# Issuing the next head pair's q and k transposes one group per block, in blocks 0, 1 and 2

## The chip, the cores and the metric

The kernel runs on one core of one Trainium2 chip. The metric is the device time of one execution in microseconds (us), as a median over runs. The engines are TensorE (PE), VectorE (DVE), ScalarE (ACT), GpSimd (POOL) and SyncE (SP, which here only issues DMAs).

## The reference

Rotary attention, whose result is flattened into tokens for a gated feed-forward layer (all in fp32):

```python
q_rot, k_rot = (rotate(q), rotate(k))              # q, k, v: (B 4, H 8, S 576, D 64)
scores = np.matmul(q_rot, k_rot.transpose(0, 1, 3, 2)) / np.sqrt(D)
scores = scores - np.max(scores, axis=-1, keepdims=True)
attn = np.exp(scores)
attn = attn / (np.sum(attn, axis=-1, keepdims=True) + 1e-09)
o = np.matmul(attn, v)
x = np.ascontiguousarray(o.transpose(0, 2, 1, 3)).reshape(B * S, H * D)   # (2304, 512)
g = x @ w_gate                                     # w_gate, w_val: (512, 1536)
out = (g * (1.0 / (1.0 + np.exp(-g))) * (x @ w_val)) @ w_out              # w_out: (1536, 512)
```

## The kernel before

The 32 heads are treated as 16 head pairs, p = 0 to 15. A pair has nine blocks, b = 0 to 8, so attention is 144 blocks, n = 9p + b. Blocks 0 to 7 are one 128-row tile of queries of one head of the pair (heads alternate); block 8 holds the 64 remaining rows of both heads. The feed-forward layer starts behind attention, and takes the last 60% of the span.

A number is kept as the sum of two halves, hi and lo, so that TensorE's fast pass keeps precision; every product is made of several passes over such halves.

A block goes through these steps. `scores` (L349): four matmuls into a PSUM tile `sc`, of which there are two buffers. DVE takes the row maximum from it (L364, `nmt`), ACT the exponential (L382, `E`, or `Et` for block 8, and behind it a short read of the accumulated sum). This exponential is the last reader of the `sc` buffer. PE transposes E (L425; the tails of 64 columns at L435 and L437) into a PSUM tile `tr`, of which there are three buffers; ACT casts that to the hi half (L426, `ET1h` or `ET2h`; L440 `TK1h`, `TK2h`), and DVE subtracts it to make the lo half (L427 and L441, `ET2l`, ...), which is the last reader of the `tr` buffer. Then PE multiplies by V (L465, `pv`), one half of a pair's query tiles at a time, and ACT copies the output out (L470, `Y`).

The next head pair is prepared beside that. SP loads q and k of a head pair into `X` (L175, `load_qk`; two buffers, so the load of pair p+2's `X` waits until POOL has read that of pair p). POOL rotates it (`rope`, L206 to L208) into `rot`; the last instruction of a head pair that reads `X` is its second big L207. In pair p, `qk_T` is called three times for pair p+1: once each for the 512 columns of q, the 512 of k, and the tails of both. A call is four transposes of PE (L289; two at L293 for the tails) into a `tr` buffer, a cast of ACT (L308, `N`), and a subtraction of DVE (L312). The last call also calls `qk_stack`, which issues eight DMAs on SP that copy `N` into the stacked tiles that the scores of pair p+1 read: `QK` (L319 and L320 for the first head, L322 and L323 for the second), `QZ` (L321, L324) and `BD` (L325, L326). Block 0 of pair p+1 needs the first head's part, block 1 the second's.

In which block of a pair the three calls are made is a row of the plan, `PLAN["qk"]`: one row for pair 0, one for pair 1 and one for pairs 2 and later. `PLAN["qkw"]` says what each call treats: for pairs from 1 on, the tails, then q, then k. The step that reads them:

```python
    def qk(n, p, b):
        w, bs = P["qkw"][min(p, 2)], P["qk"][min(p, 2)]
        if p + 1 < NP:
            for i in range(3):
                if bs[i] == b:
                    at.qk_T(p + 1, w[i], i == 2)
```

`load_qk(p + 3)` is called in block 2 of pairs 2 to 5 and in block 0 of pair 1 and of pairs 6 to 12 (L1065), ahead of the block's steps. The instructions of PE, ACT and DVE are ordered by a list scheduler with a model of their times; those of POOL stand as written all through attention, those of SP as written up to block 47 and by the scheduler from then on (pair 5 begins with block 45).

Of the kernel before, what the change touches and what calls it, by code (L numbers as in the profile page):

```python
# [28 lines left out]
    trb=3,  # L29
    warm=[9, 0, 1, 2, 0, 1],  # L30
    order=["qk", "scores", "trans", "pv", "exp", "evac", "rstore", "rope", "tails", "conv", "x", "conv1", "vsplit"],
    qk=[[3, 4, 6], [1, 2, 3], [0, 0, 1]],
    qkw=[[0, 2, 1], [2, 0, 1], [2, 0, 1]],
    tails=[4, 0],
    pv=[1, 6, 5, 3, 7, 8, 2, 7, 3],
# [1471 lines left out]
```

## Time and profile before

| | |
|---|---|
| time, median of 3 runs | 690.47 us (690.37 to 690.92) |
| time of the profiled execution | 690.11 us |
| its span in the trace | 688.3 us, so 1.8 us lie outside the span |
| busy share of the span | PE 98%, DVE 85%, POOL 68%, ACT 62% |
| attention's scores run from, to | 19.2 us, 272.2 us |

PE's share counts a matmul as busy until its modelled end, so a short wait of PE can lie hidden in it; waits are better read from the distance between the starts of its instructions than from idle time. Times in the rows are microseconds from the start of the span.

### The profile page before, as it was taken

To read this page: it belongs to the slowest core of one execution; us is meant where nothing else is said; L and a number is where in the kernel's file an instruction comes from. 1 tells how busy PE (TensorE), PEld (TensorE's weight loads), DVE (VectorE), ACT (ScalarE), POOL (GpSimd) and SP (SyncE) were. 2 spreads that over 40 slices of the span, in tenths; PEclk is the share of its full clock that TensorE was granted. 3 is DMA by queue.
4 is the path that set the end of the run, shared out by engine and by line. 5 is a ranking of instruction groups with operands and counts; after the bars stand their busy time and mean duration, and the time that the engine had idled before them with its cause. 6 is when DMAs were issued, how large, how long until landed. Compare 5 with 4: busy or idle time off the path is not lost. (4 is left out here: it accounts for less than half of the span.)

```text
span 688.3 us, 12675 instructions
## 1 busy us (share of the span) xinstructions
PE 677.4 (98%) x4414; PEld 664.3 (97%) x4414; DVE 582.4 (85%) x883; ACT 424.2 (62%) x873; POOL 470.1 (68%) x475
## 2 busy tenths in 40 slices
PE   7999999999999999999999999999999999999998
PEld 6899999999999999999999999999999999999997
DVE  5888898888888888979988898988999599877683
ACT  5899988888888888555543434424435375344341
POOL 8899799999999985998889588677784720000000
PEclk9999999999999999999999999999999999999999
DMA  6897999889988879791214345354464797627101
GB/s 195 185 248 205 218 225 243 208 206 243 246 206 208 220 189 285 187 235 70 90 58 164 122 141 204 130 187 150 161 212 163 264 317 252 207 74 247 47 24 69
DMA packets 78784, 125.76 MB, mean 183 GB/s; under 512 B 16880, under 2 KB 55680, under 8 KB 78720
## 3 DMA queue, kind: packets, MB, share of 16 engines
q1 hardware_dynamic: 75248, 118.77, 60.6%
q10 hardware_dynamic: 3472, 6.18, 2.4%
q8 instruction: 35, 0.57, 0.4%
q14 instruction: 29, 0.24, 0.1%
HBM read 66.91 MB, written 33.10 MB: 145 GB/s over the span
## 5 line engine op out<-in xcount | busy, mean ns | idle before, releaser
L364 DVE TENSOR_REDUCE nmt<-sc 128x1 f32<-128x576 f32 x144 | 108.2, 751 | 20.3 <-PE sc L349 18.9
L382 ACT ACTIVATE E<-sc,nmt 128x576 f32<-128x576 f32 x128 | 97.5, 761 | 1.7 <-DVE nmt L364 1.6
L425 PE MATMUL tr<-ident,E 128*128 128x128 f32 x512 | 77.1, 274 | 0.4 <-DVE ET1l L427 0.2
L425 PEld LDWEIGHTS tr<-ident,E 128*128 128x128 f32 x512 | 61.2, 141 | 3.4 <-PE tr L289 1.3
L1472 PE MATMUL ch<-dW,dO 128*128 128x384 f32 x216 | 63.8, 337 | 0.2 <-DVE dW L1420 0.2
L206 POOL TENSOR_TENSOR t<-X,tab 128x256 f32<-128x256 f32 (+2 forms) x94 | 54.4, 600 | 9.4 <-DMA X<-in_qk_dram 5.8
L349 PE MATMUL sc<-QK 128*128 128x288 f32 x240 | 58.7, 325 | 1.4 <-ACT E L382 0.6
L426 ACT CAST ET2h<-tr 128x512 fp32r<-128x512 f32 x80 | 47.2, 590 | 14.0 <-PE tr L425 13.7
L427 DVE TENSOR_TENSOR ET2l<-tr,ET2h 128x512 fp32r<-128x512 f32 x80 | 53.1, 682 | 2.1 <-ACT ET2h L426 2.0
L349 PE MATMUL sc<-N,QZ 128*128 128x288 f32 x240 | 51.3, 296 | 0.0
L695 POOL TENSOR_TENSOR W<-WF,W 128x1024 fp32r<-128x1024 f32 x20 | 48.1, 2409 | 3.8 <-ACT W L695 3.7
L208 POOL TENSOR_TENSOR rot<-rot,t 128x512 f32<-128x512 f32 (+2 forms) x47 | 47.0, 999 | 3.7
L427 DVE TENSOR_TENSOR ET1l<-tr,ET1h 128x512 fp32r<-128x512 f32 x64 | 43.0, 685 | 7.0 <-ACT ET1h L426 6.7
L207 POOL TENSOR_TENSOR rot<-X,tab 128x512 f32<-128x512 f32 (+2 forms) x47 | 47.0, 1001 | 0.0
L1472 PE MATMUL ch<-dH,dO 128*128 128x384 f32 x156 | 45.5, 337 | 0.0
L426 ACT CAST ET1h<-tr 128x512 fp32r<-128x512 f32 x64 | 36.9, 597 | 13.1 <-PE tr L425 13.1
L842 PE MATMUL ch<-T2h,W 128*128 128x384 f32 x160 | 44.2, 337 | 0.0
L842 PE MATMUL ch<-T0h,W 128*128 128x384 f32 x160 | 44.2, 337 | 0.0
L842 PE MATMUL ch<-T1h,W 128*128 128x384 f32 x160 | 44.1, 336 | 0.0
L465 PE MATMUL pv<-ET2h,VS 128*128 128x320 f32 x128 | 40.8, 329 | 1.1 <-ACT ET2h L426 0.9
L349 PEld LDWEIGHTS sc<-QK 128*128 128x128 f32 x240 | 36.9, 190 | 4.3 <-ACT E L382 4.1
L1472 PEld LDWEIGHTS ch<-dW,dO 128*128 128x128 f32 x216 | 39.8, 188 | 0.5 <-DVE dW L1420 0.5
(349 smaller groups left out, 2300.7 us busy)
## 6 DMA issues: line engine op xcount, KB each, us to landing
QK<-N SPq DMA_DIRECT2D x64, 288.0 KB, 4.3
hd<-sg SPq DMA_DIRECT2D x14, 768.0 KB, 3.3
dB<-hd SPq DMA_DIRECT2D x8, 1152.0 KB, 7.3
X<-in_qk_dram SPq DMA_DIRECT2D x15, 576.0 KB, 5.6
yd<-Y SPq DMA_DIRECT2D x31, 256.0 KB, 5.7
raw<-in_moe_w_gate_dram SPq DMA_DIRECT2D x12, 512.0 KB, 3.7
raw<-in_moe_w_val_dram SPq DMA_DIRECT2D x12, 512.0 KB, 4.0
Xab<-yd SPq DMA_DIRECT2D x32, 192.0 KB, 4.9
```

Of the source, the lines that this page charges most:

```text
L206: e.tensor_tensor(out=sel(t2, u), in0=sel(x, w), in1=tb(Sn, u), op=ALU.mult)
L207: e.tensor_tensor(out=o, in0=x, in1=tb(C, slice(0, D)), op=ALU.mult)
L208: e.tensor_tensor(out=o, in0=o, in1=t2, op=ALU.add)
L349: nc.tensor.matmul(ps[:, g, 0:288], l, rr[:, o + g * 288:o + (g + 1) * 288], start=(x == 0), stop=(x == len(terms) - 1))
L364: nc.vector.tensor_reduce(out=nmcol, in_=ps[:, :, 0:288], axis=AX.XY, op=ALU.max, negate=True)
L382: nc.scalar.activation(out=E.rearrange("p (a b) -> p a b", a=2), in_=ps[:, :, 0:288], func=ACTF.Exp, bias=nmcol, scale=1.0, accum_out=self ...
L425: nc.tensor.transpose(ps[:, c], E[:, o + c * 128:o + (c + 1) * 128], self.ident)
L426: nc.scalar.copy(dst[0], src)
L427: nc.vector.tensor_tensor(out=dst[1], in0=src, in1=r32(dst[0]), op=ALU.subtract)
L695: return [lambda: self.nc.scalar.copy(h, f), lambda: le.tensor_tensor(out=l, in0=f, in1=r32(h), op=ALU.subtract)]
L842: nc.tensor.matmul(acc, l[:, w, c * 128:(c + 1) * 128], r, start=(n == 0 and k not in ONTO), stop=(n == 5), skip_group_check=True)
L1472: nc.tensor.matmul(ps, l, r[:, f], start=(new and f == 0 and x == 0), stop=(f == NFP - 1 and x == 2), skip_group_check=True)
```

## The change

The three calls of `qk_T` go to blocks 0, 1 and 2, one each, in every pair from 1 on. In pair 1 each stands one block earlier than before; in pairs 2 and later the tails stay in block 0, q goes from block 0 to block 1, and k, with the eight DMAs of `qk_stack`, from block 1 to block 2.

```diff
-    qk=[[3, 4, 6], [1, 2, 3], [0, 0, 1]],
+    qk=[[3, 4, 6], [0, 1, 2], [0, 1, 2]],
```

The number of instructions is the same on each engine; what differs is their order within attention. The steps of a block work ahead: in block n the scores and the exponential are those of block n+1. Order of PE in block 0 and 1 of a pair, before (the first row is the last product by V that belongs to the block ahead; `sc<-QK` with `sc<-N,QZ` are one block's scores, here of blocks 1, 2 and 3; `Et` is block 8 of the pair ahead):

```order
L465 MATMUL pv<-TK1l,VS_115 128x256
L349 MATMUL sc<-QK_112 128x288 x2
L349 MATMUL sc<-N_111,QZ_114 128x288 x2
L289 MATMUL tr<-ident,rot 128x128 x4
L425 MATMUL tr<-ident,Et 128x128 x4
L349 MATMUL sc<-QK_112 128x288 x2
L349 MATMUL sc<-N_111,QZ_114 128x288 x2
L435 MATMUL tr<-ident,E 128x128 x2
L437 MATMUL tr<-ident,Et 128x2x64
L349 MATMUL sc<-QK_112 128x288 x2
L349 MATMUL sc<-N_111,QZ_114 128x288 x2
L289 MATMUL tr<-ident,rot 128x128 x4
```

and PE of the change at the same place:

```order
L465 MATMUL pv<-TK1l,VS_115 128x256
L293 MATMUL tr<-ident,rot 128x128 x2
L349 MATMUL sc<-QK_112 128x288 x2
L349 MATMUL sc<-N_111,QZ_114 128x288 x2
L425 MATMUL tr<-ident,Et 128x128 x4
L349 MATMUL sc<-QK_112 128x288 x2
L349 MATMUL sc<-N_111,QZ_114 128x288 x2
L435 MATMUL tr<-ident,E 128x128 x2
L437 MATMUL tr<-ident,Et 128x2x64
L465 MATMUL pv<-ET2h,VS_115 128x320
L289 MATMUL tr<-ident,rot 128x128 x4
L349 MATMUL sc<-QK_112 128x288 x2
```

The q transposes went from behind the scores of block 1 to just ahead of those of block 3, and one product by `ET2h` now stands ahead of them; the k transposes, in the last row of before, follow later, behind the scores of block 4.

Order of ACT there, before (from the copy of the block-8 tails to the second `ET1h`):

```order
L385 COPY Et<-Et 128x64
L382 ACTIVATE E,sumt<-sc,nmt 128x576
L470 COPY Y_2460<-pv 128x256
L308 CAST N_91<-tr 128x512
L382 ACTIVATE E,sumt<-sc,nmt 128x576
L426 CAST ET2h<-tr 128x4x2x64
L440 CAST TK2h<-tr 128x384
L382 ACTIVATE E,sumt<-sc,nmt 128x576
L308 CAST N_91<-tr 128x512
L426 CAST ET1h<-tr 128x4x128
```

and ACT of the change:

```order
L385 COPY Et<-Et 128x64
L382 ACTIVATE E,sumt<-sc,nmt 128x576
L470 COPY Y_2460<-pv 128x256
L308 CAST N_91<-tr 128x3x64
L426 CAST ET2h<-tr 128x4x2x64
L382 ACTIVATE E,sumt<-sc,nmt 128x576
L440 CAST TK2h<-tr 128x384
L382 ACTIVATE E,sumt<-sc,nmt 128x576
L308 CAST N_91<-tr 128x512
L426 CAST ET1h<-tr 128x4x128
```

The cast of q (128x512) no longer stands ahead of the exponential of block 1 (the second `L382` row); the casts of the tails (128x3x64) and of `Et` do.

Order of SP, the piece of the difference in pair 5, where the stack of pair 6 is issued:

```order
-L319 DMA QK_92<-N_91 64x2x576
-L320 DMA QK_92<-N_91 64x2x576
-L321 DMA QZ_94<-N_91 64x512
-L322 DMA QK_92<-N_91 64x2x576
-L323 DMA QK_92<-N_91 64x1152
-L324 DMA QZ_94<-N_91 64x512
-L325 DMA BD_93<-N_91 64x2x64
-L326 DMA BD_93<-N_91 64x2x64
-L175 DMA X<-in_qk_dram 128x1152
-L489 DMA yd_57<-Y_1561 128x2x256
-L490 DMA yd_57<-Y_1561 128x2x64
-L175 DMA X<-in_qk_dram 128x1152
```

```order
+L175 DMA X<-in_qk_dram 128x1152 x2
+L319 DMA QK_92<-N_91 64x2x576
+L320 DMA QK_92<-N_91 64x2x576
+L321 DMA QZ_94<-N_91 64x512
+L322 DMA QK_92<-N_91 64x2x576
+L323 DMA QK_92<-N_91 64x1152
```

The two loads of `X` went from behind the stack to ahead of it. In pairs 2 to 4 one load of `X` does the same. In pair 6 the load of head pair 10's `X` goes from behind the four `QK` DMAs to ahead of them; from pair 7 on it stands behind them in both.

## Rows read from the trace of the kernel before

**Rows 1.** Windows, a steady stretch: busy us by engine, granted clock, DMA share, GB/s.

```profile
150.00:200.00 50.00, 49.68 (x394) 48.45 (x393) 43.73 (x71) 44.39 (x114) 47.82 (x57) 1.00 0.92 236
```

**Rows 2.** Timeline of PE, start of pair 11: start, duration, engine, line, tiles, count.

```profile
195.50 0.43 PE L349 MATMUL sc<-QK 128*128 128x288 f32 x2
...
197.68 0.27 PE L437 MATMUL tr<-ident,Et 128*128 128x128 f32 x1
198.05 0.52 PE L349 MATMUL sc<-QK 128*128 128x288 f32 x2
...
198.68 0.60 PE L289 MATMUL tr<-ident,rot 128*128 128x128 f32 x4
199.03 0.39 PE L465 MATMUL pv<-ET2h,VS 128*128 128x320 f32 x1
199.40 0.63 PE L425 MATMUL tr<-ident,E 128*128 128x128 f32 x4
...
201.04 0.42 PE L349 MATMUL sc<-QK 128*128 128x288 f32 x2
```

**Rows 3.** Timeline of PE in pair 0, the same sequences without a wait.

```profile
29.12 0.27 PE L437 MATMUL tr<-ident,Et 128*128 128x128 f32 x1
29.15 0.50 PE L349 MATMUL sc<-QK 128*128 128x288 f32 x2
...
33.03 0.39 PE L465 MATMUL pv<-TK2l,VS 128*128 128x320 f32 x1
33.27 0.49 PE L425 MATMUL tr<-ident,E 128*128 128x128 f32 x3
```

**Rows 4.** Timeline of ACT, start of pair 11; brackets show idle time and releaser.

```profile
196.68 0.59 ACT L308 CAST N<-tr 128x512 fp32r<-128x512 f32 x1 [0.19 <-PE tr L289]
197.16 0.75 ACT L382 ACTIVATE E<-sc,nmt 128x576 f32<-128x576 f32 x1
197.80 0.20 ACT L382 ACTIVATION_READ_ACCUMULATOR E<-sc,nmt 128x1 f32 x1
```

**Rows 5.** Timeline of DVE, start of pair 11.

```profile
196.24 0.76 DVE L364 TENSOR_REDUCE nmt<-sc 128x1 f32<-128x576 f32 x1
...
198.57 0.68 DVE L427 TENSOR_TENSOR ET2l<-tr,ET2h 128x512 fp32r<-128x512 f32 x1
```

**Rows 6.** Timeline of PE: a stall in pair 4, scores of pairs 6 and 7.

```profile
81.58 0.41 PE L465 MATMUL pv<-ET2h,VS 128*128 128x320 f32 x1 [0.88 <-ACT ET2h L426]
...
113.02 0.43 PE L349 MATMUL sc<-QK 128*128 128x288 f32 x2
...
127.03 0.51 PE L349 MATMUL sc<-QK 128*128 128x288 f32 x2
...
129.48 0.42 PE L349 MATMUL sc<-QK 128*128 128x288 f32 x2
```

**Rows 7.** Timeline of SP, DMA issues of pairs 3 and 6.

```profile
74.46 0.59 SPq L175 DMA_DIRECT2D X<-in_qk_dram  x1
...
118.81 0.61 SPq L319 DMA_DIRECT2D QK<-N  x1
...
121.10 1.27 SPq L323 DMA_DIRECT2D QK<-N  x1
123.66 0.33 SPq L175 DMA_DIRECT2D X<-in_qk_dram  x1
```

**Rows 8.** Timeline of POOL: the rope of head pairs 6, 7 and 8.

```profile
80.12 0.60 POOL L206 TENSOR_TENSOR t<-X,tab 128x64 f32<-128x64 f32 x2 [3.76 <-DMA X<-in_qk_dram]
...
103.95 1.29 POOL L207 TENSOR_TENSOR rot<-X,tab 128x512 f32<-128x512 f32 x1
...
122.33 1.30 POOL L207 TENSOR_TENSOR rot<-X,tab 128x512 f32<-128x512 f32 x1
```

**Rows 9.** DMA issues in 109 to 110: count, KB each, us to landing.

```profile
X<-in_qk_dram SPq DMA_DIRECT2D x1, 576.0 KB, 4.4
```

**Rows 10.** All DMAs that write tile QK.

```profile
DMA to landing us min/median/max: 3.2/4.3/7.1
```

## The prediction

> **What bounds the kernel now.** I read the page first, for the shares of the engines, and then the windows of a steady stretch of attention: in 50 us PE is busy 49.68 at a granted clock of 1.00, POOL 47.82, and the DMA engines carry 236 GB/s at a share of 0.92 [rows 1]. So PE sets the pace at its full clock, POOL and the DMAs follow closely, and DVE and ACT have some room. A change that adds and removes no instruction can only win back PE's waits. These lie hidden in its busy time, so the timeline is to be read by the distance between starts. From the scores of block 1 in pair 7 (129.48) to those in pair 11 (195.50) there are four pairs in 66.02 us, 16.5 each [rows 2, 6].
>
> In each such pair there are two waits at its start. **The first:** the lone transposes of L437 start at 197.68 and the scores behind them at 198.05, 0.37 later; without a wait the same two rows stand 0.03 apart [rows 2, 3]. That is 0.34. The scores waited for their `sc` buffer, which the exponential of block 1 frees. On ACT that exponential starts at 197.16, directly behind the cast of q (196.68), which itself had to wait 0.19 for its transposes; its maximum on DVE was done at 196.24 + 0.76 = 197.00 [rows 4, 5]. So the q cast, not the maximum, is what came last. **The second:** `pv` starts at 199.03, the transposes behind it at 199.40, 0.37 against 0.24 without a wait [rows 2, 3]. That is 0.13. They waited for a `tr` buffer, which the subtraction of `ET2l` frees at 198.57 + 0.68 = 199.25 [rows 5]; the q group took one of the three buffers, and the block-8 group stood behind it. Together 0.47 us a pair, which is all that this change can give in a steady pair.
>
> **The change, part by part.** No instruction is added or removed on any engine, so the feed-forward part costs the same and shifts with attention's end. Four things move.
>
> *The q group, in pairs from 2 on, to behind the scores of block 2.* Ahead of the third scores (of block 3) PE now has the same work as before and one product more. Before, they were ready 0.34 ahead of 198.05, that is 2.21 after the scores of block 1 at 195.50; with the 0.24 of that product [rows 3] it is 2.45. When is the buffer free? On ACT the cast of block 8 takes the place of the q cast, behind transposes that stand in the same place, so I let the exponential start as before, 197.16 - 195.50 = 1.66 after those scores; it released the third scores 198.05 - 197.16 = 0.89 later [rows 2, 4]. So the buffer is free at 2.55, and the wait is 0.10 where it was 0.34: 0.24 saved. The second wait goes, because the block-8 group now comes first and its buffer is free long before: 0.13 saved. The sum is 0.37 a pair. The bounds are 0 (the exponential comes 0.24 later, behind the tail cast that now also stands ahead of it) and 0.47 (the exponential follows its maximum at once).
>
> *Which pairs keep it.* Pairs 8 and 12 have the extra transposes and copies of the row sums in the same place, with a wait of their own; I count nothing for them. Pairs 15 and 0 prepare nothing or are unchanged. Pairs 7, 9, 10, 11, 13 and 14 remain, six: 6 x 0.37 = 2.2, bounds 0 and 6 x 0.47 = 2.8.
>
> *The k group and the stack, one block later.* k's transposes stood at 198.68 and now follow the scores of block 4, at 201.04 with some 0.5 for those [rows 2]; less the 0.35 of their own length and the 0.37 saved, that is about 201.04 + 0.5 - 0.35 - 0.37 - 198.68 = 2.1 us later. The second head's last `QK` DMA is issued at 121.10 in pair 6 and needed at 129.48 [rows 6, 7]: 8.38 ahead, less 2.1 is 6.3. Such a DMA lands after 4.3 in the median and 7.1 at most [rows 10]. So 2.0 of cover are left in the median case, and the worst costs 0.8 in one pair. I take nothing, since the six pairs' slack repeats and the median fits; without that cover each pair would lose what it lacks.
>
> *The loads of X, ahead of the stack, up to pair 6.* This is the part with a sign that must be weighed. First what it gives: head pair 6's X was issued at 74.46, behind a stack, and POOL stood 3.76 for it at 80.12 [rows 7, 8]. Issued ahead, this wait goes; since POOL is busy 47.82 in 50, all that follows on POOL comes about 3.76 earlier. Then what it costs: a load of X can wait for POOL to have read the buffer's old contents, and on SP all that is queued behind it waits too. For head pair 10's load that read ends at 122.33 + 1.30 = 123.63, and the load went at 123.66 [rows 7, 8]. With POOL's gain it goes at 119.9. It lands 4.4 later [rows 9], at 124.3. The four `QK` DMAs of pair 7 now stand behind it. At 236 GB/s [rows 1] each of 288 KB takes 294,912 B / 236 GB/s = 1.25 (an estimate): the second is there at 126.8, the fourth at 129.3. The scores that read them start at 127.03 and 129.48 [rows 6]. So if these transfers queue behind X, only 0.2 us of what PE may have gained in pairs 1 to 6 survives pair 7. If they go beside X, the last is issued 2.29 + 0.6 (the distance from 118.81 to 121.10, and X's own issue) after 119.9 and lands 4.3 later, at 127.1: then 2.4 survive. For pair 6 the load of head pair 9 waits for 103.95 + 1.29 = 105.24, less 3.76 is 101.5; with 4.4 and four times 1.25 the last lands at 110.9, against 113.02 [rows 6, 8], so there 2.1 could survive. Since the DMA engines are at 0.92, I take the first case, 0.2, and round it to nothing.
>
> The Trainium skill, "DMA: Bandwidth & Descriptors", section "Anatomy of one DMA", gives for a transfer issued by GpSimd 2.0 us plus the bytes at 436 GB/s, which for X's 589,824 bytes is 3.35 us (an estimate); the row above has 4.4 on SP's queue. By that figure X lands 1.05 earlier and about 1.2 us of the gain of pairs 1 to 6 would survive, for 687.1 us; the measured row decides here.
>
> **The sum.** The profiled execution took 690.11, the median is 690.47; a saving does not depend on which, and the profiled one would come to 690.11 - 2.2 = 687.9. From the median: 690.47 - 2.2 = 688.3 us.
>
> **The rivals.** *Full gain.* The transfers of pair 7 go beside X and the early pairs' waits are won too, such as the 0.88 of PE at 81.58 [rows 6]. For it: POOL's 3.76 goes for certain if X is early. Against it: the DMA share of 0.92. It gives 2.2 + 2.4 = 4.6, so 685.9 us.
>
> *The wait only moves.* The q cast leaves the exponential of block 1, but it and the k cast now stand ahead of later exponentials, and each is 0.59 long on ACT [rows 4]. If one of these exponentials then frees its `sc` buffer 0.37 too late, the pair gains nothing; the tail cast ahead of block 1's exponential works the same way. For it: two `sc` buffers leave every score behind the exponential two blocks ahead. Against it: later in the pair products by V stand between two scores, 1.6 us from 199.40 to 201.04 [rows 2], so that an exponential has more time there than at the start. It gives 690.5 us.
>
> *Slower: pair 7 waits behind X.* If POOL does not come 3.76 earlier, because it meets another wait on the way to the rope of head pair 8, the load goes at 123.66 as before, X lands at 128.1 and the fourth `QK` at 133.1, 3.6 after 129.48 [rows 6, 7, 9]. With the steady saving that is 690.47 + 3.6 - 2.2 = 691.9 us. It decides the sign from the point where the load goes later than about 119.9 + 0.2 + 2.2 = 122.3. For it: the load has to wait on SP. Against it: POOL's work itself does not change. The same page of the Trainium skill, in the same section, says that a DMA engine does not wait on semaphores and the sequencer that issues does. The trace agrees: the load's issue stands 0.03 behind POOL's last read [rows 7, 8], and all that is behind it on SP stands too.
>
> **How the numbers follow.** The forecast has a chance of 0.36, the full gain 0.15, the moved wait 0.29, the wait behind X 0.20. The time is that of the first, 688.3. About 0.2% (1.4 us) is what a measurement of this kernel can tell from no change: faster is below 689.1, slower above 691.85. The forecast's own range, with its bounds of 0 to 0.47 a pair, is 687.7 to 690.5, and a part of it, with most of the moved wait, falls in "same"; full gain and nearly all the rest of the forecast make faster 0.50, same 0.31, slower 0.19. The range of 8 in 10 runs from the full gain to the slower rival, 685.6 to 691.9, and leaves out half of the latter and little at the lower end.
>
> **What would show it.** Right: in pairs 9 to 14 the third scores stand about 0.13 behind the transposes ahead of them, the period falls from 16.5 to 16.1, POOL's rope of head pair 6 starts without a wait, and PE waits a little for `QK` DMAs in pair 7, where the trace's gain is back at nothing. Wrong: scores that wait for an exponential elsewhere in the pair, waits of PE for a DMA in pairs 3 to 6 or in the steady ones, or a load of X later than 122.3.

## The result and the profile after

The changed kernel takes 696.68 us (median of 6 runs, 695.2 to 699.35), where the kernel before takes 690.66 in the same comparison (6 runs, 689.76 to 691.17). The ratio is 1.0093 [1.0073, 1.0113]: slower by 0.9%, some 6.0 us, where 688.3 was forecast and 691.9 was the upper end. The profiled execution took 697.94 us, 7.8 more than the profiled one of before.

From the page: the span, the shares of the engines, and the group of the scores that read `QK`, with the idle time ahead of it.

```profile
span 696.2 us, 12731 instructions
...
PE 677.3 (97%) x4414; PEld 665.4 (96%) x4414; DVE 585.9 (84%) x883; ACT 426.7 (61%) x873; POOL 470.8 (68%) x475
...
L349 PE MATMUL sc<-QK 128*128 128x288 f32 x240 | 58.9, 326 | 6.3 <-DMA QK<-N 5.6
```

PE stood 5.6 us for `QK` DMAs. The prediction had wanted to see at most a small wait of this kind, in pair 7. The steady stretch answers to [rows 1]:

```profile
150.00:200.00 50.00, 49.13 (x393) 48.24 (x392) 44.35 (x73) 44.81 (x114) 47.28 (x57) 1.00 0.87 225
```

The clock is the same, and PE carries as much work (393 matmuls in 50 us, before 394); so the steady stretch is not where the time went. The timeline of PE shows where:

```profile
94.09 0.40 PE L349 MATMUL sc<-N,BD 128*128 128x288 f32 x1 [1.18 <-ACT E L382]
...
100.63 0.44 PE L435 MATMUL tr<-ident,E 128*128 128x128 f32 x2 [0.85 <-DVE ET2l L427]
...
131.60 0.50 PE L349 MATMUL sc<-QK 128*128 128x288 f32 x2 [1.34 <-DMA QK<-N]
...
152.33 0.27 PE L400 MATMUL tr<-ident,rt 128*36 128x128 f32 x1 [0.41 <-DVE rt L393]
...
153.20 0.41 PE L435 MATMUL tr<-ident,E 128*128 128x128 f32 x2 [0.45 <-DVE N L312]
...
183.63 0.38 PE L349 MATMUL sc<-QK 128*128 128x288 f32 x1
...
199.85 0.50 PE L349 MATMUL sc<-QK 128*128 128x288 f32 x2
...
201.73 0.41 PE L465 MATMUL pv<-ET2h,VS 128*128 128x320 f32 x1
201.98 0.60 PE L289 MATMUL tr<-ident,rot 128*128 128x128 f32 x4
202.46 0.53 PE L349 MATMUL sc<-QK 128*128 128x288 f32 x2
...
266.97 0.50 PE L349 MATMUL sc<-QK 128*128 128x288 f32 x2 [3.49 <-DMA QK<-N]
```

Setting the same scores of the two traces side by side gives how much later each stands (differences of the unrounded times):

| scores | before | the change | later by |
|---|---|---|---|
| block 8 of pair 0 | 23.34 | 24.20 | 0.86 |
| block 1 of pair 4 | 78.46 | 79.12 | 0.66 |
| block 2 of pair 5 | 97.48 | 100.94 | 3.45 |
| block 1 of pair 7 | 129.48 | 133.98 | 4.50 |
| block 1 of pair 14 | 245.08 | 249.40 | 4.33 |
| block 0 of pair 15 | 259.08 | 266.97 | 7.9 |

The first 0.86 is not the change's: at that point both kernels have run the same instructions, and over all the traces below this start lies between 0.24 earlier and 0.86 later than before. Behind it there are three places of loss. The end of pair 4 and the start of pair 5 cost 2.8, of which the first two waits above are 2.0. The start of pair 7 costs about 1.4. The start of pair 15 costs 3.6, nearly all of it the last wait. In between, seven pairs win only 0.17 net, and the feed-forward part adds nothing in this trace. The profiled execution is 1.3 slower than the median, so not all of these are there each time; the section on five traces of one order, below, shows which are.

The DMA issues of SP, first the last `QK` DMA and the first L772 of the kernel before, then the change at pair 7 and at the last stack:

```profile
252.63 1.34 SPq L323 DMA_DIRECT2D QK<-N  x1
...
260.90 0.57 SPq L772 DMA_DIRECT2D raw<-in_moe_w_gate_dram  x1
```

```profile
122.46 0.35 SPq L175 DMA_DIRECT2D X<-in_qk_dram  x1
122.91 0.62 SPq L319 DMA_DIRECT2D QK<-N  x1
...
255.47 0.35 SPq L772 DMA_DIRECT2D raw<-in_moe_w_gate_dram  x1
255.88 1.61 SPq L772 DMA_DIRECT2D raw<-in_moe_w_val_dram  x1
257.58 0.62 SPq L319 DMA_DIRECT2D QK<-N  x1
258.29 0.62 SPq L320 DMA_DIRECT2D QK<-N  x1
...
261.75 1.06 SPq L630 DMA_DIRECT2D R<-rd  x1
```

L772 (`rawload`) loads a 512 KB piece of the feed-forward weights. Before, the last `QK` DMAs went at 250.32 to 252.63 and the first L772 at 260.90, behind them and behind `R<-rd`, the row sums' reciprocals (L630). Now two of these loads stand ahead of the `QK` DMAs. The DMAs issued from 257.5 to 261, with KB each and the median us to landing:

```profile
QK<-N SPq DMA_DIRECT2D x4, 288.0 KB, 8.7
```

Before, the same four landed after 5.6 (here and below, the median of those of the four whose landing the trace has: two before, four in the change). The scores of pair 15 could have started at 266.97 - 3.49 = 263.48. The second `QK` DMA of its first head was issued at 258.29 and landed 8.5 later, at 266.8; the scores started at 266.97.

For the end of pair 4, DVE before, then DVE (with the subtraction of k's lo half in pair 14 as the last row), POOL and ACT of the change:

```profile
88.99 1.20 DVE L754 TENSOR_SCALAR raw<-raw 128x512 uint32<-128x512 uint32 x1
90.11 0.74 DVE L364 TENSOR_REDUCE nmt<-sc 128x1 f32<-128x576 f32 x1
```

```profile
90.67 1.78 DVE L754 TENSOR_SCALAR raw<-raw 128x512 uint32<-128x512 uint32 x1
92.37 1.41 DVE L364 TENSOR_REDUCE nmt<-sc 128x1 f32<-128x576 f32 x2
...
256.10 0.69 DVE L312 TENSOR_TENSOR N<-tr,N 128x512 fp32r<-128x512 f32 x1 [0.30 <-ACT N L308]
```

```profile
90.59 1.58 POOL L279 TENSOR_TENSOR VS<-VR,VS 128x640 fp32r<-128x640 f32 x1
```

```profile
93.21 0.74 ACT L382 ACTIVATE E<-sc,nmt 128x576 f32<-128x576 f32 x1 [0.62 <-DVE nmt L364]
```

A step of the weight conversion (L754, 1.78 us) stands ahead of two maxima; the exponential waits for its maximum, and PE's scores of block 8 wait for the exponential. Before, that step (88.99, 1.20 us) was followed by one maximum alone, and PE did not wait. The length of the step is POOL's doing. Alone it takes 0.41. Here it starts 0.08 behind the start of POOL's L279, which ends at 90.59 + 1.58 = 92.17, and it ends 0.28 after that, at 92.45. In the 16 traces this step stands 52 times in and just behind attention; 32 times it took over 0.44, and each time it ended 0.28 after the end of the POOL instruction that ran when it started.

POOL, the start and the end of ropes, and a wait between two of them, answers to [rows 8]:

```profile
76.59 0.60 POOL L206 TENSOR_TENSOR t<-X,tab 128x64 f32<-128x64 f32 x2
...
101.21 1.28 POOL L207 TENSOR_TENSOR rot<-X,tab 128x512 f32<-128x512 f32 x1
...
109.16 0.73 POOL L278 TENSOR_SCALAR VS<-VR 128x640 fp32r<-128x640 f32 x1 [1.55 <-PE pv L465]
...
121.15 1.29 POOL L207 TENSOR_TENSOR rot<-X,tab 128x512 f32<-128x512 f32 x1
```

POOL's wait of 3.76 for the `X` of head pair 6 is gone. The last read of head pair 7's `X` comes 2.7 us earlier, that of head pair 8's only 1.2 (123.63 before, now 122.44), where 3.76 was forecast: POOL now waits twice for PE's products, 0.81 at 89.78 and 1.55 at 109.16.

### The profile page after: what moved, and what is told of

Same layout as the page of the kernel before. It is cut to its first block, busy times and chain, and to the rows that moved or that the text cites. A ratio compares the mean times of both kernels' runs of the same rounds, so it can differ in the third digit from the quotient of the medians.

```text
span 696.2 us, 12731 instructions
## 1 busy us (share of the span) xinstructions
PE 677.3 (97%) x4414; PEld 665.4 (96%) x4414; DVE 585.9 (84%) x883; ACT 426.7 (61%) x873; POOL 470.8 (68%) x475
## 4 chain that ended last, share of the span: by engine, by line
PE 78%; DVE 8%; DMA 7%; POOL 3%; issue 2%; ACT 2%; SPq 0%; ACTq 0%; DVEq 0%; POOLq 0%
PE ch L842 28%; PE ch L1472 14%; PE pv L465 10%; PE sc L349 9%; PE ch L794 7%; PE tr L425 6%; DMA QK<-N 3%; PE tr L289 2%; DMA yd<-Y 2%; DVE dB L1410 1%; DVE nmt L364 1%; DMA dO<-od 1%; ACT E L382 1%; PE tr L435 1%; DVE dO L1391 1%
## 5 line engine op out<-in xcount | busy, mean ns | idle before, releaser
L364 DVE TENSOR_REDUCE nmt<-sc 128x1 f32<-128x576 f32 x144 | 108.0, 751 | 27.8 <-PE sc L349 26.9
L382 ACT ACTIVATE E<-sc,nmt 128x576 f32<-128x576 f32 x128 | 97.1, 759 | 7.9 <-DVE nmt L364 7.9
L427 DVE TENSOR_TENSOR ET2l<-tr,ET2h 128x512 fp32r<-128x512 f32 x80 | 53.7, 680 | 2.2 <-ACT ET2h L426 1.8
L207 POOL TENSOR_TENSOR rot<-X,tab 128x512 f32<-128x512 f32 (+2 forms) x47 | 47.0, 999 | 0.0
L427 DVE TENSOR_TENSOR ET1l<-tr,ET1h 128x512 fp32r<-128x512 f32 x64 | 42.8, 684 | 4.1 <-ACT ET1h L426 3.8
```

The source lines that it names most:

```text
L364: nc.vector.tensor_reduce(out=nmcol, in_=ps[:, :, 0:288], axis=AX.XY, op=ALU.max, negate=True)
L382: nc.scalar.activation(out=E.rearrange("p (a b) -> p a b", a=2), in_=ps[:, :, 0:288], func=ACTF.Exp, bias=nmcol, scale=1.0, accum_out=self ...
L427: nc.vector.tensor_tensor(out=dst[1], in0=src, in1=r32(dst[0]), op=ALU.subtract)
```

## The experiments

**Theory:** the loss has two main causes. The scheduler puts weight loads ahead of the last stack, supposedly since SP is idle there while it waits for k, which comes one block later; and the end of pair 4 has a DVE step in a worse place. **Rivals:** k one block later is enough by itself to make the `QK` DMAs late; or the loss lies at the end in `R<-rd`, which feeds POOL; or the early loss comes from `X`.

All kernels have the old row in the plan, so pair 0 and the pairs not named are as before; one line of the step `qk` gives the named pairs the new row:

```diff
-        w, bs = P["qkw"][min(p, 2)], P["qk"][min(p, 2)]
+        w, bs = P["qkw"][min(p, 2)], [0, 1, 2] if p in PAIRS else P["qk"][min(p, 2)]
```

Below only `PAIRS` or, where pair 14 gets a row of its own, the expression is shown.

### The last stack: pair 14 alone

**Pair 14 as before, all else changed.**

```diff
+ p in (1, 2, 3, 4, 5, 6, 7, 8, 9, 10, 11, 12, 13)
```

> The changed kernel, but pair 14 (which prepares pair 15) keeps its old row: k and the stack in block 1, so that SP issues the four QK copies ahead of the two weight loads (L772). Theory W (the two weight loads ahead of the QK copies cost the 3.49 us wait at 266.97): the wait goes, 696.7 - 3.5 = 693.2 us. Rival K (the stack issued one block later is enough to be late): also 693.2, since both are undone. Rival A (PE is late at pair 15 for what piled up before, and would wait for something else): 696.7.

It took 698.21, ratio 1.0112 [1.0096, 1.0128]. The wait of pair 15 is gone, yet nothing is won. The scheduler has now put both L772 and the first two loads of L780, more weights, between the stack and `R<-rd`, which goes at 263.37, and POOL waits for it:

```profile
274.40 1.02 POOL L645 TENSOR_TENSOR Xab<-Xab,R 128x384 f32<-128x384 f32 x1 [6.04 <-DMA R<-rd]
```

The loss comes back in the feed-forward part, which needs what POOL makes here. An old row in pair 14 does not bring the old order of SP back.

**Pair 14 with k in block 2, tails and q in block 1.** No weight load stands ahead of the stack here.

```diff
+ [0, 1, 2] if 0 < p < 14 else [1, 1, 2] if p == 14 else P["qk"][0]
```

> The changed kernel with the row 1, 1, 2 in pair 14: k and the stack still in block 2, as changed, but the order that comes of it has no weight load ahead of the QK copies. W: the wait goes nearly whole, 693.2 us, within 0.5. K: the wait of some 3.5 us stays, 696.7.

It took 697.08, ratio 1.0094 [1.008, 1.0109]. By its time alone this speaks for the rival, k's delay. By its trace it does not: the `QK` DMAs land after 5.3 in the median and no scores of pair 15 wait for them. So k in block 2 is not enough for that wait. The time goes elsewhere: POOL waits 7.24 for `Xab<-yd`, DVE 1.90 for POOL ahead of a maximum (273.56), and the scores at 276.43 wait 1.69 for the exponential behind it.

**Pair 14 with tails and q in block 0, k in block 2.** One weight load stands ahead of the stack.

```diff
+ [0, 1, 2] if 0 < p < 14 else [0, 0, 2] if p == 14 else P["qk"][0]
```

> The changed kernel with the row 0, 0, 2 in pair 14: k and the stack in block 2, with one weight load (512 KB) ahead of the QK copies in place of two. W: the wait falls by what one load takes, 524,288 B at 236 GB/s = 2.2 us, to about 1.3: 694.5 us. K: 696.7.

It took 693.9, ratio 1.0048 [1.0036, 1.006]. PE in pair 15:

```profile
262.34 0.50 PE L349 MATMUL sc<-QK 128*128 128x288 f32 x2 [0.92 <-DMA QK<-N]
...
264.98 0.50 PE L349 MATMUL sc<-QK 128*128 128x288 f32 x2 [0.26 <-DMA QK<-N]
```

**Only pair 14 changed.** Two weight loads stand ahead of the stack.

```diff
+ p in (14,)
```

> The kernel before, with the changed row in pair 14 alone: two weight loads ahead of the QK copies, all else as before. W and K: 690.5 + 3.5 - 0.3 = 693.7 us, and one wait of PE for QK at the start of pair 15. A: 690.2, the saving of one pair.

It took 693.02, ratio 1.003 [1.002, 1.004], so this pair alone costs 2.1 us. PE in pair 15 waits 1.22 + 0.92 = 2.14:

```profile
262.85 0.50 PE L349 MATMUL sc<-QK 128*128 128x288 f32 x2 [1.22 <-DMA QK<-N]
...
264.98 0.50 PE L349 MATMUL sc<-QK 128*128 128x288 f32 x2 [0.92 <-DMA QK<-N]
```

**Pair 14 with q and k both in block 1.** `QK` and `R<-rd` both go ahead of all weight loads.

```diff
+ [0, 1, 2] if 0 < p < 14 else [0, 1, 1] if p == 14 else P["qk"][0]
```

> The changed kernel with the row 0, 1, 1 in pair 14: the order that comes of it on SP has the QK copies and both R<-rd loads ahead of all four weight loads, as the kernel before has it. Theory S (the loss at the end of attention is the order of SP's transfers: weights ahead of QK, or weights ahead of R): neither wait, 696.7 - 3.5 = 693.2 us. Rival: any kernel with the row in pair 13 loses some 6 us at the end of attention whatever SP's order is, 696 to 698, as in the two runs with k back in block 1 or with 1, 1, 2.

It took 693.28, ratio 1.005 [1.003, 1.007]: about 3 us of the 6 are back (1.0093 - 1.005 = 0.43%), as expected. SP, the last `QK` DMA, the first `R<-rd` and the first weight load, and behind it the four `QK` DMAs with their median time to landing:

```profile
256.10 1.38 SPq L323 DMA_DIRECT2D QK<-N  x1
...
260.58 0.62 SPq L630 DMA_DIRECT2D R<-rd  x1
...
265.15 0.55 SPq L772 DMA_DIRECT2D raw<-in_moe_w_gate_dram  x1
```

```profile
QK<-N SPq DMA_DIRECT2D x4, 288.0 KB, 5.7
```

Together (cover is the time from the issue of the first `QK` DMA to where the first scores of pair 15 were otherwise ready, that is their start less their wait):

| kernel | weight loads ahead | landing, median | cover | PE's waits |
|---|---|---|---|---|
| the change | 2 | 8.7 | 5.9 | 3.49 |
| only pair 14 | 2 | 9.4 | 8.65 | 1.22, 0.92 |
| 0, 0, 2 | 1 | 8.2 | 7.85 | 0.92, 0.26 |
| 0, 1, 1 | 0 | 5.7 | 8.1 | none |
| 1, 1, 2 | 0 | 5.3 | 7.0 | none |
| pairs 4 and 5 as before (0, 1, 2 in pair 14) | 0 | 4.2 | 7.1 | none |

In the 13 traces without loads ahead (before and twelve experiments, some of them below) these DMAs land after 4.2 to 7.2 in the median, with loads ahead after 8.2 to 9.4. That, and not k's block, makes the wait: in 1, 1, 2 and in the last run of all, with pairs 4 and 5 as before, k stands in block 2 too, and PE does not wait. The cover, which is not the same in the three kernels with loads ahead although k stands in block 2 in all of them, sets how much of the landing shows. In the change itself k's lo half was done at 256.10 + 0.69 = 256.79 and SP was busy with the second load until 255.88 + 1.61 = 257.49, so 0.8 of the cover went there too.

**Five traces of one order.** The change and the four kernels above that keep its rows up to pair 13 (pair 14 as before; 1, 1, 2; 0, 0, 2; 0, 1, 1) have the same instructions in the same order on every engine up to the scores of block 0 of pair 14. So up to there their traces are five executions of one program, and show what belongs to the order and what to the execution. The loss from block 1 of pair 4 to block 2 of pair 5 is 2.75 to 2.80 in all five. Pairs 7, 10 and 11 win 0.22 to 0.30 each in all five. The wait of pair 7 is in the change's trace alone: in the other four `X` stands ahead of the stack as well, but the first `QK` DMA lands after 5.5 to 5.9 (7.4 in the change), and PE does not wait. Pair 8 loses 0.61 in the change and wins 0.16 or 0.17 in the other four; pair 12 loses 0.38 to 0.61 in four and wins 0.17 in one. And PE waits 0.61 to 1.33 for `QK` at the start of pair 2 in four of the five.

**Only pair 13 changed.**

```diff
+ p in (13,)
```

> The kernel before with the changed row in pair 13 alone. On SP the only part of note that follows is that the two loads R<-rd of pair 15 go from ahead of the four weight loads (L772 twice, L780 twice) to behind them. Theory R (as in the run with pair 14 as before, POOL waits for R and the feed-forward part starts late): 690.7 - 0.3 + 5 to 6 = 695.5 to 696.5 us, with a wait of POOL for R of 5 to 6 us near 272. Rival: that loss belonged to pair 14's row alone, and this gives 690.4.

It took 697.73, ratio 1.0096 [1.0081, 1.011]: one steady pair, which should have won 0.37, costs 6.8 us. Attention ends 0.26 earlier than before; all is lost behind it. SP, and POOL:

```profile
256.83 0.54 SPq L772 DMA_DIRECT2D raw<-in_moe_w_gate_dram  x1
...
258.97 1.67 SPq L780 DMA_DIRECT2D raw<-in_moe_w_gate_dram  x2
261.63 1.26 SPq L630 DMA_DIRECT2D R<-rd  x2
```

```profile
272.66 1.02 POOL L645 TENSOR_TENSOR Xab<-Xab,R 128x384 f32<-128x384 f32 x1 [6.01 <-DMA R<-rd]
```

Before, `R<-rd` went at 257.04, ahead of all of these. From 300 to 350 us PE is now busy 46.62 of 50, before 50.00. So the feed-forward start hangs on the same order of SP, by a second thread.

### The steady pairs

**Pairs 7, 9, 10 and 11.**

```diff
+ p in (7, 9, 10, 11)
```

> The kernel before with the changed row in pairs 7, 9, 10 and 11 alone; SP's order around the end of attention is that of before. The prediction's step for a steady pair (0.37 us saved) gives 690.7 - 1.5 = 689.2 us; what the traces of the changed kernels show for these pairs (about 0.25 a pair) gives 689.7; a rival by which the k stack one block later makes QK late in a steady pair gives a loss, above 690.7.

It took 691.85, ratio 1.0011 [1.0003, 1.002]: no gain. Pairs 7 and 9, each behind an unchanged pair, win 0.43 and 0.44; pairs 10 and 11 win 0.02 each. Pairs 8 and 12, unchanged behind changed ones, give back 0.47 and 1.06; the longest wait of PE there stands at 213.38:

```profile
213.38 0.44 PE L425 MATMUL tr<-ident,Et 128*128 128x128 f32 x2 [0.81 <-DVE ET2l L427]
```

So this kernel does not isolate the steady saving: it has borders that the change has not. No run shows that saving by its time; it is read from the traces of the kernels with all these pairs changed.

**Pairs 8 and 12**, with the row sums:

```diff
+ p in (8, 12)
```

> The kernel before with the changed row in pairs 8 and 12 alone, those with the row sums. Prediction: nothing, 690.7. By the changed kernel's trace each loses 0.5 to 0.6 (PE waits for the reciprocal and for the tails' subtraction): 691.8. By two of the other traces a pair of this kind gains 0.17: 690.4.

690.53, ratio 0.9997 [0.9985, 1.0009]: nothing, as the prediction had it.

**Pairs 2, 3, 8 and 12.**

```diff
+ p in (2, 3, 8, 12)
```

> The kernel before with the changed row in pairs 2, 3, 8 and 12, the ones in which the traces of the changed kernels show no loss; SP's order around the end of attention is that of before. By those traces 0.4 us for pairs 2 and 3 together and 0.2 each for 8 and 12: 690.9 - 0.8 = 690.1 us. Rival (each place where the two rows meet costs some 0.5, as in the run of four steady pairs): 691.9.

691.35, ratio 1.0013 [1.0003, 1.0023]: no gain here either.

### The early pairs

**Pairs 1 to 5.**

```diff
+ p in (1, 2, 3, 4, 5)
```

> The kernel before with the changed row in pairs 1 to 5 alone (the X loads go ahead of the stack there, and the weight conversion of DVE meets other neighbours in pairs 4 and 5). Theory E (the order of DVE and ACT in pairs 4 and 5 loses what the traces of the changed kernels show, some 2.4 us by the start of pair 6): 693.1 us, with PE waiting for the exponential at the end of pair 4 and for ET2l at the start of pair 5, and no wait for QK. Theory of the prediction (a gain that pair 7 takes back): 690.7. A rival by which the X loads make QK late: waits of PE for QK in pairs 2 to 6.

693.45, ratio 1.0049 [1.0032, 1.0066]: the size that was expected. The two waits at the end of pair 4 are there with the lengths that they have in the change, 1.18 at 95.60 and 0.85 at 102.14. The profiled execution, at 695.3 slower than the median, also has two waits for `QK` in pair 2, of 1.29 and 1.08.

**Pair 1.**

```diff
+ p in (1,)
```

> The kernel before with the changed row in pair 1 alone, where it issues the stack of pair 2 one block earlier. Rival of theory E (the QK copies issued earlier meet the loads of X and V and land later): a wait of PE for QK of 0.8 to 2.4 us at the start of pair 2, 691.5 to 693. Theory E: 690.9 or a little less.

690.91, ratio 1.0008 [1.0, 1.0017]: the wait for pair 2's `QK` is not due to pair 1's row alone.

**Pairs 4 and 5.**

```diff
+ p in (4, 5)
```

> The kernel before with the changed row in pairs 4 and 5 alone. Theory E (all of the early loss lies where DVE converts weights, pairs 4 and 5): 690.9 + 2.4 = 693.3 us, with PE waiting for an exponential near 94 and for ET2l near 100. Rival (it lies at pair 2, where QK landed late): 690.9.

693.83, ratio 1.0051 [1.0039, 1.0063]. The size is the expected one and the mechanism is not: DVE makes no one wait. SP and PE show another:

```profile
98.59 6.97 SPq L175 DMA_DIRECT2D X<-in_qk_dram  x2
105.66 0.62 SPq L319 DMA_DIRECT2D QK<-N  x1
```

```profile
112.70 0.50 PE L349 MATMUL sc<-QK 128*128 128x288 f32 x2 [2.06 <-DMA QK<-N]
```

With pair 3 unchanged, POOL keeps its wait for the `X` of head pair 6 (80.03, 3.82 us), so it reads the `X` of head pair 7 until 103.92 + 1.29 = 105.21; the second of the two loads waits on SP until then, and the stack behind it. That is the prediction's slower rival, one pair earlier than it was placed. The wait also has an echo in the granted clock (third number from the end of a row), in which the products by V start 0.21 apart instead of 0.12; block 0 of pair 6 stands 2.13 later than before, block 1 3.41:

```profile
108.00:112.70 4.70, 2.64 (x24) 2.43 (x22) 2.94 (x6) 3.70 (x10) 4.45 (x6) 1.00 1.04 247
112.70:117.00 4.30, 4.30 (x22) 4.24 (x23) 1.97 (x3) 2.01 (x6) 4.14 (x7) 0.61 0.84 189
```

**The change with pair 5 as before**, on top of 0, 1, 1 in pair 14:

```diff
+ [0, 1, 2] if 0 < p < 14 and p != 5 else [0, 1, 1] if p == 14 else P["qk"][min(p, 2)]
```

> The changed kernel with the row 0, 1, 1 in pair 14 (693.3 us when run by itself) and the old row in pair 5. If the early loss lies in pair 4 (PE waits 1.18 us for an exponential at its end, behind the weight conversion on DVE): 693.3 as before. If it lies in pair 5 (the two X loads ahead of the stack, the wait for ET2l at its start): 690.5 to 691.

692.8, ratio 1.0033 [1.0022, 1.0044]. Both early waits of PE stay:

```profile
93.98 0.40 PE L349 MATMUL sc<-N,BD 128*128 128x288 f32 x1 [1.18 <-ACT E L382]
...
100.51 0.44 PE L425 MATMUL tr<-ident,Et 128*128 128x128 f32 x2 [0.84 <-DVE ET2l L427]
```

So pair 5's row does not cause them. The time is lower than with pair 5 changed (1.005), but the two intervals overlap.

**The change with pairs 4 and 5 as before.** This moves SP's order at the end too: `QK` and `R<-rd` go ahead of the weights without an edit there.

```diff
+ p in (1, 2, 3, 6, 7, 8, 9, 10, 11, 12, 13, 14)
```

> The changed kernel with the old row in pairs 4 and 5 (pair 14 keeps the changed row). The order that comes of it on SP has the QK copies of pair 15 and both R loads ahead of all weight loads, and the load of X behind the stack in pairs 4 and 5. Theory S and E together (the loss is that of pairs 4 and 5, 2.5 to 3.4 us, and that of SP's order at the end, 3.4): 696.7 - 3.4 - 2.5 to 3.4 = 690 to 691 us. Rival (row 0, 1, 2 itself loses in pair 14, whatever SP's order): 693.5 to 694.

692.04, ratio 1.002 [1.001, 1.003]: with both places undone the loss falls from 0.93% to 0.2%. Pair 14 keeps the row 0, 1, 2 here; no load stands ahead of its stack, which lands after 4.2, and the scores of pair 15 start without a wait, 0.14 later than before (259.08):

```profile
259.22 0.51 PE L349 MATMUL sc<-QK 128*128 128x288 f32 x2
```

The last 1.3 us appear behind that: at block 8 of pair 15 the shift is 1.26, with waits of PE for ACT of 0.28, 0.21 and 0.74 at 272.63, 274.44 and 276.69. No version was faster than the kernel before.

## Why the prediction was wrong

**The step that failed** is part of "The k group and the stack, one block later": "I take nothing, since the six pairs' slack repeats and the median fits". The cover was sized well. For the first head, [rows 6, 7] give 127.03 - 118.81 - 2.1 = 6.1, and 5.9 was measured in pair 14, the 0.8 for SP's second load being in it. The landing was not: 8.7 where 4.3 in the median and 7.1 at most were taken from [rows 10]. The 7.1 was itself the last stack's, whose fourth DMA (252.63 above) landed after 7.08 before the change: a first sign that this stack is not like the others. The six pairs do not repeat in pair 14, because there two weight loads, which the scheduler had placed later before, stand ahead of the stack. The prediction looked at SP's order in pairs 2 to 7 alone, and its list of pairs that keep the gain counted 13 and 14 as steady. The runs put this place at about 3 of the 6 us (0, 1, 1 in pair 14), and the trace at 3.6.

**The second failure** is in the same count: pairs 1 to 6 were given a gain that pair 7 takes back, so nothing. They lost. With 0, 1, 1 in pair 14 the ratio is 1.005, with pairs 4 and 5 undone 1.002, so these are worth 0.3%, some 2 us (roughly: the two intervals just meet; the five traces of one order have 2.8). The waits there are for DVE and ACT, which the prediction had as engines with "some room"; a 1.78 us step ahead of two maxima uses that room up at once. That it is pair 4's row, together with those of 1 to 3, follows from four runs: the waits stand with pairs 1 to 5 changed and with pair 5 undone, and not with 4 and 5 alone, nor with 4 and 5 undone. The traces say how the two come together. With rows 1 to 3 changed POOL comes earlier (its L279 went at 93.51 before and goes at 90.59 in the change), and with pair 4's row as well DVE's L754 falls on it. With pairs 4 and 5 as before L754 goes ahead of it and takes 0.42. No run changes the length of L754 without the order, so their shares of the wait stay open. The prediction counted POOL's 3.76 as a gain with a price on SP alone, and gave it none on DVE.

**The steady saving** had the right mechanism and a size somewhat too large. In pair 10 to 11 the period is 199.85 - 183.63 = 16.22, where before the same two scores stand 195.50 - 179.05 = 16.45 apart: 0.23 for a forecast of 0.37 (pairs 7, 9, 11 and 13 win 0.26 or 0.27 in this trace). The third scores stand 0.48 behind the transposes, which take 0.35, so they wait 0.13 (forecast 0.10, before 0.34, [rows 2]); the second wait is gone, 201.98 - 201.73 = 0.25 against 0.24 unstalled [rows 3]. The forecast's two steps thus give 0.21 + 0.12 = 0.33, and some 0.1 goes elsewhere in the pair. In this trace pairs 8 and 12 lost most of that again: a wait of 0.41 for the reciprocal of the row sums and one of 0.45 for q's lo half in pair 8, 0.31 and 0.45 in pair 12. That is not fixed by the order: in the five traces of one order a pair of this kind lost wherever the scaling of the row sums (L392) took 0.98 to 1.23, and won wherever it took 0.17 or 0.18. It is long when POOL is in the middle of an instruction, as told in the last section.

**X ahead of the stack** came about, but not as priced. POOL's 3.76 went, and the load went 0.02 after POOL's last read (121.15 + 1.29 = 122.44, load 122.46). But that is 2.6 later than the 119.9 of the sum, since POOL met two waits for PE on the way, and later than the 122.3 that was named as a sign of being wrong. `X` then landed after 6.7, where 4.4 was taken from [rows 9]; before, the load at the same place (123.66) took 5.7. In this trace pair 7 waited 1.34 for the DMAs behind it; in four other traces of the same order it did not wait. So the sum's first case, by which pair 7 takes the early gain back, is not what decided: there was no gain to take back, and the price was paid in one execution of five.

**The rivals.** The full gain falls. The moved wait did not come about as described (the casts ahead of exponentials), though DVE's wait at pair 4 is one of its kind. The slower rival is true of the kernel with pairs 4 and 5 alone, and in small of pair 7 in the one trace; its condition, that POOL meets another wait, held. Its 691.9 was nearest to the result, but for another reason than the one that cost most.

**Open:** the last 0.2%, and why pair 2's `QK` DMAs land after 7 to 9.6 us in some traces (0.80 of PE in the change): the kernels with rows 1 to 3 changed have that wait in seven traces of eight, the others in none. A version in which SP's order alone is pinned, with all the new rows kept, was not tried; pairs 4 and 5 as before comes nearest to it.

## What to carry to other kernels

A saving read off a steady stretch holds only where the neighbours are the steady ones. Where a scheduler orders a DMA queue, read the order of that queue at each place where other traffic joins it, such as the last pairs ahead of the next stage: a transfer that fills an idle hole can delay the transfer behind it by 3 us (5.6 to 8.7 here). Work that one engine does earlier can lengthen a step of another that falls beside it, as POOL's did to DVE's. And read the trace of an experiment, not only its time: two edits that took the wait away were as slow as the change, for reasons further on.

## What the hardware showed that was not expected

The last stack's four `QK` DMAs, of the same size in all kernels, landed after 4.2 to 7.2 us (median of the four) with no weight load ahead of them on SP, and after 8.2 to 9.4 with one or two; one load alone has most of the effect.

A wait of PE of 2.06 us (pairs 4 and 5) was followed by a granted clock of 0.61 in the next 4.3 us, a mixture of the two levels of 1.2 and 2.4 GHz, and the clock was back at 1.00 from 117 to 125. In the changed kernel the wait of 3.49 us was followed by 1.00 in the 4.3 us behind it. So the length of the wait alone does not tell whether the clock falls.

The same DVE instruction can take very different times: the scaling of the row sums (L392, 128x36) 0.35 us before and 1.23 in the change, and the conversion step L754 1.20 and 1.78. The traces show with what: POOL. L754 alone takes 0.41, and ends 0.28 after the end of the POOL instruction in all 32 cases of 52 in which it took longer. L392 alone takes 0.17, and ends 0.04 after the end of a POOL instruction in all 43 cases of 64 in which it took over 0.22; in pair 8 of the change it ran from 150.08 to 151.31, beside POOL's L207 from 149.98 to 151.27. The maxima (L364) and the subtractions (L427) of DVE in the same stretch keep their 0.74 to 0.76 and 0.67 to 0.69. The profile counts that time as busy, not as a wait.
